# Attention one batch at a time: four kv heads in one transfer of 64 KB a partition and one softmax, where two heads were handled at a time

## The chip, the cores and the metric

The kernel runs on one core of a Trainium2 chip. A core has a matmul engine (TensorE, in the profile PE, and PEld for its weight loads), a vector engine (VectorE, DVE), a scalar engine (ScalarE, ACT), GpSimd (POOL), and SyncE (SP), which here only issues transfers; 16 DMA engines move data from HBM into SBUF, the on-chip memory of 128 partitions. Matmul results go to PSUM, eight banks of 512 float32 a partition. The metric is the device time of one execution in microseconds, the median of several runs; less is better.

## The reference: what is computed

One decode step of a transformer block for 8 batch rows, all weights and caches in bf16. Width D = 1024; 32 query heads on 4 kv heads of 128; a cache of 8192 keys for each batch row and kv head; a gated MLP of F = 3584 with a ReLU gate.

```
mod = (silu(c) @ w_mod) in six parts: sa, ca, ga, sb, cb, gb
h   = layernorm(x) * (1 + ca) + sa
q   = h @ wq                                  # 8 x 32 x 128
s   = q . k_cache * 128**-0.5                 # for each batch row: 32 x 8192
o   = softmax(s) @ v_cache                    # 8 x 32 x 128
x   = x + ga * (o @ wo)
h   = layernorm(x) * (1 + cb) + sb
x   = x + gb * ((relu(h @ W_gate) * (h @ W_up)) @ W_down)
```

K and V are 67.1 MB each; the weights together are 51.4 MB. Each byte is used once.

## The kernel before, in words

**Order and waits.** The kernel is written by hand on a small recorder, `Prog`. `P.op` records an operation for one engine with the ranges that it reads and writes; from these the recorder derives every semaphore wait. Each engine runs its operations in the order recorded. An entry of several matmuls counts as one operation: others can wait for its end alone.

**Transfers.** All large loads go through SyncE's queue, in one order fixed by the list `stream`: w_mod, wq, then K and V of pair 0, K and V of pair 1, and so on, then wo, W_gate, W_up, W_down. `pump` (L381) is called after each recorded TensorE operation. It takes the head of the list if its target range in `arena`, 128 KB a partition, has been read, and records the issue (L393), which then waits for the last readers of that range. `P.held` keeps the range of a K or V transfer from being taken until `free` names the operation that ends its use. The arena is a ring: K or V of a pair takes 32 KB a partition, so four such transfers fit, and K and V have two places each.

**The attention loop** (L683) goes over M = 16 pairs of kv heads, two pairs for one turn of the hardware loop. For a pair m:

- `kt_part` (L586): VectorE transposes an eighth of K in 32x32 blocks into one of four slots of the tile `kt`; the first one waits for K's transfer.
- `qk_part` (L597): four matmuls multiply it with the query weights `qpad` into PSUM; four eighths fill one bank.
- `rowmax` (L609), `spread` (L613, L615), `headmax` (L620, L623): the maximum of the scores of a head, spread over the partitions by a matmul.
- `expo` (L629): ScalarE takes the exponent of two banks, 128x1024, and its sum.
- `p_turn` (L636): VectorE transposes the result in two halves of 64 partitions straight into `pT`, whose zeros keep the two heads of a pair apart.
- `make_qpad` (L578), on GpSimd: query weights of pair m + 2, two places in turn.
- `pv` (L646): 32 matmuls of 512 columns, two at a time on the two halves of the array's columns; waits for V's transfer.
- `fold` (L654, L657), `fold_pe` (L663), `keep` (L668): four masked sums on VectorE, a matmul and a copy bring the result into `oacc`. They are recorded in the middle of pair m + 1, between its transposes and its softmax.

So while TensorE runs PV of one pair, VectorE transposes K of the next, and V of pair m is released by the rowmax of pair m + 1.

**After the loop** come the division by the sums (L706 to L714), turns of the result (L723 to L733), the wo matmuls (L743), the second layernorm (L489 to L508), the gate and up matmuls (L774), and W_down (L793), each of which waits for its part of the weights.

Of the kernel before, what the change touches and what calls it, by code (L numbers as in the profile page):

```python
# [263 lines left out]
def bass_adaLN_cond__gqa_block_cached__glu_gated_reglu__decode_kernel(nc, A_x, A_k_cache, A_v_cache, A_wq, A_wo, B_x, B_W_gate, B_W_up, B_W_down, c, w_mod, out):  # L264
# [11 lines left out]
    SLOT = 8192  # L276
    RING = 16 * 4096
# [13 lines left out]
    with ExitStack() as es:  # L291
# [9 lines left out]
        ktb = sb("kt", [128, NKT * 2048], dt.bfloat16)  # L301
# [5 lines left out]
        jm = sb("jm", [128, 2, J], dt.float32)  # L307
        jms = sb("jms", [128, 2 * J], dt.float32)
        jmp = sb("jmp", [128, 2, J], dt.float32)
        im = sb("im", [128, 4], dt.float32)  # L310
# [10 lines left out]
        M = N // 2  # L321
        qR = sb("qR", [128, 4, M, J], dt.bfloat16)
        rq = sb("rq", [128, 2, 128], dt.bfloat16)
        mq = sb("mq", [128, 4], dt.bfloat16)
        qpad = sb("qpad", [128, 2, 4, 152], dt.bfloat16)
        prb = sb("prb", [128, 1024], dt.bfloat16)
        pT = sb("pT", [128, 2, 32, 2, 32], dt.bfloat16)
        negm = sb("negm", [128, 4], dt.float32)
        mj = sb("mj", [128, 2 * J], dt.float32)
        mjt = sb("mjt", [128, 2 * J], dt.float32)  # L330
        bias = sb("bias", [128, 2], dt.float32)
        lall = sb("lall", [128, M], dt.float32)
        lx = sb("lx", [128, M, 2 * J], dt.float32)
        om = sb("om", [128, Dh], dt.float32)
        oacc = sb("oacc", [128, M + 1, 2 * J], dt.float32)
# [21 lines left out]
        for t in "kv":  # L357
            for i in range(2):
                sems[(t, i)] = E(nc.semaphore("%s_%d" % (t, i)))

        def at(m):

            return m if P.turn is None else 2 * P.turn + m % 2
# [12 lines left out]
        stream, place, cursor = [], {}, [0]  # L376

        def load(key, src, n):
            stream.append((key, src, n))

        def pump():  # L381
            while stream:
                key, src, n = stream[0]
                lo = cursor[0] if cursor[0] + n <= RING else 0
# [3 lines left out]
                cursor[0] = lo + n  # L388
                place[key] = lo
                dst = arena[:, lo:lo + n]  # L390
                if len(src.shape) == 3:
                    dst = dst.rearrange("p (a n) -> p a n", a=src.shape[1])
                P.op("sp", lambda e, dst=dst, src=src: e.dma_start(dst, src), writes=[slot_r(lo, lo + n)], dma=True,  # L393
                     own=(key[0], key[1] % 2) if key[0] in "kv" else None)
# [12 lines left out]
        for i in range(2):  # L407
            load(("wq", i), wq_src[:, 2 * i * SLOT:2 * (i + 1) * SLOT], 2 * SLOT)
# [166 lines left out]
        def make_qpad(m):  # L575
            if m >= M:
                return
# [261 lines left out]
```

## Time and profile before

| | |
|---|---|
| runs, us | 437.17, 445.93, 437.15; median 437.17 |
| profiled execution, its own time | 436.92 us |
| its span (first to last instruction) | 435.6 us |
| TensorE, VectorE, ScalarE, GpSimd busy | 277.4, 265.8, 29.9, 14.5 us |
| bytes read | 185.6 MB, 426 GB/s over the span |
| granted TensorE clock, mean | 0.81 |

A row of the groups reads: line, engine, operation, output <- inputs, shape, count | busy us, mean ns of one | idle time of the engine just before and what ended most of it. A row of the timeline reads: start us, duration us, engine, line, operation, names, shapes, count, with the idle time before it and what ended it in brackets. A row of the windows gives for one stretch the busy time of each engine with its number of instructions, the granted share of the TensorE clock, the busy share of the DMA engines and their GB/s. Line numbers are those of the kernel before.

### The profile page before, as it was taken

Reading aid. Unit: us, or ns where it says so; the run is one execution under the profiler, and the core shown is the slowest. Engines: PE = TensorE matmul, PEld = TensorE weight load, DVE = VectorE, ACT = ScalarE, POOL = GpSimd, SP = SyncE. Lnnn points to the kernel's source line nnn. Section 1 sums busy time; section 2 is a strip of 40 time slices with the busy share of each in tenths; the row PEclk is TensorE's granted clock in tenths of the full one; section 3 lists DMA queues with packets and bytes.
Section 4 is the critical chain, followed back from the end, with each engine's and each line's share of the span. In section 5 each row is a group of like instructions: output and inputs, shape, how many; then the busy total and the mean of one; then the engine's idle time right before and its main releaser. Section 6 shows DMA issues by size and latency. Waiting matters only on the chain.

```text
span 435.6 us, 3869 instructions
## 1 busy us (share of the span) xinstructions
PE 277.4 (64%) x1643; PEld 120.8 (28%) x1483; DVE 265.8 (61%) x377; ACT 29.9 (7%) x62; POOL 14.5 (3%) x32
## 2 busy tenths in 40 slices
PE   0415238659595958768595958768595958636437
PEld 0100002324242423324242333324142323334105
DVE  1503058777686877777778777677788776253020
ACT  2000010110101010010101010010101010110000
POOL 7000000000000000000000000000000000000000
PEclk9966668697888869696978969696987969668858
DMA  9999999999999999999999999999999999999995
GB/s 373 438 444 433 429 433 433 434 430 432 433 433 433 433 433 433 433 433 433 433 433 433 433 433 433 433 433 433 433 433 433 433 433 433 423 429 444 428 420 233
DMA packets 7078, 185.74 MB, mean 426 GB/s; under 512 B 832, under 2 KB 928, under 8 KB 1312
## 3 DMA queue, kind: packets, MB, share of 16 engines
q1 hardware_dynamic: 6944, 185.61, 98.9%
q8 instruction: 5, 0.08, 0.1%
q10 hardware_dynamic: 128, 0.04, 0.0%
q14 instruction: 1, 0.01, 0.0%
HBM read 185.63 MB, written 0.02 MB: 426 GB/s over the span
## 4 chain that ended last, share of the span: by engine, by line
PE 46%; DVE 20%; issue 13%; DMA 6%; ACT 0%; SPq 0%
PE ps L646 22%; PE ps L597 18%; DVE kt L586 9%; DMA arena<-in_B_W_down_dram 6%; DVE negm L609 5%; PE ps L615 2%; PE ps L663 2%; PE ps L743 1%; DVE om L657 1%; DVE mj L620 1%; PE ps L774 1%; DVE mjt L623 1%; DVE negm L613 1%; DVE kt L733 0%; DVE lx L706 0%
## 5 line engine op out<-in xcount | busy, mean ns | idle before, releaser
L586 DVE STREAM_TRANSPOSE kt<-arena 128x1024 uint32<-128x1024 uint32 x128 | 149.6, 1217 | 39.0 <-PE ps L597 26.8
L597 PE MATMUL ps<-kt,qpad 128*128 128x512 bf16 x512 | 122.4, 385 | 9.6 <-DVE kt L586 8.3
L646 PE MATMUL ps<-arena,pT 128*64 128x512 bf16 x512 | 95.4, 554 | 51.7 <-issue 51.7
L646 PEld LDWEIGHTS ps<-arena,pT 128*64 128x64 bf16 x512 | 45.5, 157 | 95.5 <-issue 91.1
L597 PEld LDWEIGHTS ps<-kt,qpad 128*128 128x128 bf16 x512 | 46.0, 97 | 84.6 <-DVE kt L586 28.7
L636 DVE STREAM_TRANSPOSE pT<-prb 64x1024 bf16<-64x1024 bf16 x32 | 39.6, 1239 | 18.1 <-ACT prb L629 17.6
L629 ACT ACTIVATE prb<-ps,bias 128x1024 bf16<-128x1024 f32 x16 | 17.8, 1113 | 293.1 <-DVE mjt L623 293.1
L609 DVE TENSOR_REDUCE negm<-ps 128x1 f32<-128x512 f32 x32 | 22.1, 692 | 12.7 <-PE ps L597 12.7
L663 PE MATMUL ps<-jmp,om 128*128 128x16 f32 x34 | 7.4, 293 | 17.0 <-DVE om L657 17.0
L657 DVE SCALAR_TENSOR_TENSOR om<-ps,im,om 128x128 f32<-128x128 f32 x51 | 17.7, 347 | 0.7
L615 PE MATMUL ps<-identf,negm 128*128 128x128 f32 x32 | 7.8, 326 | 15.6 <-DVE negm L613 15.6
L578 POOL TENSOR_TENSOR qpad<-qR,mq 128x128 bf16<-128x128 bf16 x16 | 6.3, 399 | 317.6 <-DVE pT L636 267.7
L774 PE MATMUL ps<-arena,hT 128*32 128x448 bf16 x128 | 9.4, 459 | 9.4 <-DMA arena<-in_B_W_up_dram 6.8
L544 PE MATMUL ps<-arena,hT 128*32 128x512 bf16 x64 | 7.1, 623 | 12.7 <-DMA arena<-in_A_wq_dram 12.7
L521 PE MATMUL ps<-arena,hT 128*32 128x512 bf16 x96 | 9.2, 565 | 9.2 <-DMA arena<-in_w_mod_dram 9.2
L793 PE MATMUL ps<-arena,hmT 128*32 128x256 bf16 x112 | 8.7, 320 | 5.6 <-DMA arena<-in_B_W_down_dram 5.4
L528 DVE COPY mod<-ps 128x512 f32<-128x512 f32 x2 | 1.3, 671 | 17.8 <-PE ps L521 17.8
L781 DVE TENSOR_TENSOR kt<-ps,kt 128x448 bf16<-128x448 f32 x2 | 1.2, 621 | 17.6 <-PE ps L774 17.6
L663 PEld LDWEIGHTS ps<-jmp,om 128*128 128x128 f32 x34 | 5.7, 210 | 20.5 <-DVE om L657 20.5
L615 PEld LDWEIGHTS ps<-identf,negm 128*128 128x128 f32 x32 | 4.7, 187 | 23.6 <-DVE negm L613 23.6
L555 DVE CAST kt<-ps 128x512 bf16<-128x512 f32 x1 | 0.7, 692 | 16.3 <-PE ps L544 16.3
L793 PEld LDWEIGHTS ps<-arena,hmT 128*32 128x32 bf16 x112 | 6.2, 114 | 9.0 <-DMA arena<-in_B_W_down_dram 7.6
(89 smaller groups left out, 89.2 us busy)
## 6 DMA issues: line engine op xcount, KB each, us to landing
arena<-in_A_k_cache_dram SPq DMA_DIRECT2D x16, 4096.0 KB, 21.1
arena<-in_A_v_cache_dram SPq DMA_DIRECT2D x16, 4096.0 KB, 19.0
arena<-in_A_wq_dram SPq DMA_DIRECT2D x2, 4096.0 KB, 34.9
arena<-in_A_wo_dram SPq DMA_DIRECT2D x2, 4096.0 KB, 18.0
arena<-in_B_W_gate_dram SPq DMA_DIRECT2D x2, 3584.0 KB, 15.5
arena<-in_B_W_up_dram SPq DMA_DIRECT2D x2, 3584.0 KB, 19.0
arena<-in_w_mod_dram SPq DMA_DIRECT2D x1, 6144.0 KB, 30.7
arena<-in_w_mod_dram SPq DMA_DIRECT2D x1, 5888.0 KB, 16.6
```

What stands on the lines that cost most here:

```text
L521: fns.append(lambda e, w=w, pr=pr, j=j, kk=kk: hold(e.matmul(ps[32 * j:32 * j + 32, pr, :], hT[:, kk, :], w[:, 2 * pr:2 * pr + 2, j, :], s ...
L586: P.op("dve", lambda e: e.transpose(ktb[:, to:to + QE].bitcast(dt.uint32), arena[:, lo:lo + QE].bitcast(dt.uint32)), reads=[slot_r(lo, lo ...
L597: fns.append(lambda e, t=t, r=r: e.matmul(ps[:, b, :].rearrange("p (c k) -> p c k", k=32), qpad[:, m % 2, t * 2 + r, 24 - 8 * i:152 - 8 * ...
L609: P.op("dve", lambda e: e.tensor_reduce(negm[:, h:h + 1], ps[:, b, :], AX.X, ALU.max, negate=True), reads=[bank(b)] + (free(("v", m - 1)) ...
L615: P.op("pe", lambda e: e.matmul(ps[:, 4, 0:128], negm[:, 2:3].to_broadcast([128, 128]), identf[:], start=True, stop=True), reads=[R("negm" ...
L629: P.op("act", lambda e: e.activation(prb[:], ps[:, 2 * z:2 * z + 2, :].rearrange("p h n -> p (h n)"), ACT.Exp, bias=bias[:, z:z + 1], scal ...
L636: P.op("dve", lambda e, g=g: e.transpose(pT[64 * g:64 * g + 64, z, :, g, :], prb[64 * g:64 * g + 64, :]), reads=[R("prb")] + ([R("qpad", z ...
L646: fns.append(lambda e, t=t: e.matmul(ps[64 * (t % 2):64 * (t % 2) + 64, 5, :].rearrange("p (i d) -> p i d", d=Dh), pT[:, z, t].rearrange(" ...
L657: P.op("dve", lambda e, i=i: e.scalar_tensor_tensor(out=om[:], in0=ps[:, 5, Dh * i:Dh * i + Dh], scalar=im[:, i:i + 1], in1=om[:], op0=ALU ...
L663: P.op("pe", lambda e: e.matmul(ps[:, 6 + z, 0:16], om[:], jmp[:].rearrange("p g j -> p (g j)"), start=True, stop=True), reads=[R("om"), R ...
L774: fns.append(lambda e, w=w, r=kk - r0, kk=kk, h=h, j=j, b0=b0: hold(e.matmul(ps[32 * j:32 * j + 32, b0 + h, 0:H], hT[:, kk, :], w[:, r, j, ...
L793: fns.append(lambda e, w=w, r=k - r0, k=k, i2=i2, j=j: e.matmul(ps[32 * j:32 * j + 32, 4, 0:256], hmT[:, k, 1 - i2:33 - i2], w[:, r, i2, j ...
```

## The change

Attention goes over the 8 batches in place of 16 pairs, one turn of the hardware loop each. K of all four kv heads of a batch is one transfer of 64 KB a partition (8.4 MB), V another. The arena grows to 144 KB a partition with fixed places: K at 0, a staging area of 16 KB behind it, V behind that; each of K and V has one place. GpSimd copies the last quarter of K (parts 12 to 15 of 16) into the staging area as soon as K has landed, so that K's place is free after part 11 has been transposed and the copy is done; its release is named by the first rowmax, recorded after part 12. There is one softmax maximum over four banks, two exponents (f = 0, 1), and the turn of P is one transpose of 128 partitions followed by four masked copies, which write `pT` in the place of `kt`. PV has twice as many matmuls of half as many columns. The two folds of a batch are recorded at its own end, and release V. QK of parts 0 and 1 is one recorded operation. wq is loaded in parts of six and two eighths (it was halves), gate, up and wo in one transfer each; up goes where wo lay and W_down where gate lay.

The core of the diff:

```diff
-    SLOT = 8192
-    RING = 16 * 4096
+    SLOT = Sk * G * Dh // 128
+    PART = SLOT // 16
+    STAGE, VPART, RING = SLOT, SLOT + 4 * PART, 2 * SLOT + 4 * PART
...
-        pT = sb("pT", [128, 2, 32, 2, 32], dt.bfloat16)
+        pT = ktb.rearrange("p (f c i g x) -> p f c i g x", f=2, c=32, i=2, g=G)
...
-        for i in range(2):
-            load(("wq", i), wq_src[:, 2 * i * SLOT:2 * (i + 1) * SLOT], 2 * SLOT)
-        for m in range(M):
-            for nm, t in (("k", A_k_cache), ("v", A_v_cache)):
-                load((nm, m), t[m // 2, 2 * (m % 2):2 * (m % 2) + 2].rearrange("g (p c) d -> (g p) (c d)", p=64), 2 * SLOT)
-        wo_parts = [(0, 16), (16, 32)]
...
+        wq_parts = [(0, 6), (6, 8)]
+        for i, (r0, r1) in enumerate(wq_parts):
+            load(("wq", i), wq_src[:, r0 * 4096:r1 * 4096], (r1 - r0) * 4096, 48 * D if i == 0 else STAGE)
+        for b in range(B):
+            for nm, t, lo in (("k", A_k_cache, 0), ("v", A_v_cache, VPART)):
+                load((nm, b), t[b].rearrange("g (p c) d -> (g p) (c d)", p=32), SLOT, lo)
+        load(("wo", 0), wo_src, KO * D, 0)
+        load(("gate", 0), g_src, KC * F, VPART)
+        load(("up", 0), u_src, KC * F, 0)
...
+        def kt_part(b, e):
+            lo = e * PART if e < 12 else STAGE + (e - 12) * PART
+            to = e % NKT * PART
+            P.op("dve", lambda e_: e_.transpose(ktb[:, to:to + PART].bitcast(dt.uint32), arena[:, lo:lo + PART].bitcast(dt.uint32)),
...
+        def set_aside(b):
+            lo = 12 * PART
+            P.op("pool", lambda e: e.tensor_copy(arena[:, STAGE:STAGE + 4 * PART].bitcast(dt.uint32),
+                                                 arena[:, lo:lo + 4 * PART].bitcast(dt.uint32)),
+                 reads=[R("landed"), slot_r(lo, lo + 4 * PART)], writes=[slot_r(STAGE, STAGE + 4 * PART)])
...
+        def rowmax(b, h):
+            P.op("dve", lambda e: e.tensor_reduce(negm[:, h:h + 1], ps[:, h, :], AX.X, ALU.max, negate=True),
+                 reads=[bank(h)] + (free(("k", b)) if h == 0 else []), writes=[R("negm", h, h + 1)])
...
-        def p_turn(m):
-            z = m % 2
-            for g in range(2):
-                P.op("dve", lambda e, g=g: e.transpose(pT[64 * g:64 * g + 64, z, :, g, :], prb[64 * g:64 * g + 64, :]),
+        def p_turn(b, f):
+
+            P.op("dve", lambda e: e.transpose(pd[:, f], prb[:, f]), reads=[R("prb", f, f + 1)], writes=[R("pd", 1024 * f, 1024 * f + 1024)])
+            for g in range(G):
+                P.op("dve", lambda e, g=g: e.tensor_scalar(out=pT[:, f, :, :, g, :], in0=pd[:, f].rearrange("p (c i x) -> p c i x", c=32, i=2),
+                                                           scalar1=mqf[:, g:g + 1], scalar2=None, op0=ALU.mult),
...
+        def pv(b, f):
...
+            for n in range(64):
+                h, c_, i, t = n // 32, n // 2 % 16, n % 2, n % 2
+                fns.append(lambda e, n=n, h=h, c_=c_, i=i, t=t: e.matmul(
+                    ps[64 * t:64 * t + 64, 5, 0:2 * Dh].rearrange("p (i d) -> p i d", d=Dh),
+                    pT[:, f, 16 * h + c_, i].rearrange("p g x -> p (g x)"), vv[:, f, h, c_, 2 * i:2 * i + 2],
...
+        def fold(b):
+            for i in range(2):
+                P.op("dve", lambda e, i=i: e.tensor_scalar(out=om[:, i], in0=ps[:, 5, Dh * i:Dh * i + Dh], scalar1=im[:, i:i + 1],
+                                                           scalar2=None, op0=ALU.mult),
+                     reads=[bank(5), R("im")] + (free(("v", b)) if i == 0 else []), writes=[R("om", i, i + 1)])
...
-        for m in range(M):
-            P.trip = m // 2
-            for e8 in range(8):
-                kt_part(m, e8)
-                qk_part(m, e8)
-                if e8 == 5:
-                    rowmax(m, 0)
-            fold(m - 1, 0)
-            fold(m - 1, 1)
-            rowmax(m, 1)
-            spread(m)
-            fold(m - 1, 2)
-            headmax(m)
-            expo(m)
-            fold(m - 1, 3)
-            fold_pe(m - 1)
-            keep(m - 1)
-            p_turn(m)
-            make_qpad(m + 2)
-            pv(m)
+        for b in range(B):
+            P.trip = b
+            kt_part(b, 0)
+            set_aside(b)
+            kt_part(b, 1)
+            qk_parts(b, (0, 1))
+            for e in range(2, 16):
+                kt_part(b, e)
+                qk_parts(b, (e,))
+                if e >= 12 and e < 15:
+                    rowmax(b, e - 12)
+            rowmax(b, 3)
+            headmax(b)
+            for f in range(2):
+                expo(b, f)
+            for f in range(2):
+                p_turn(b, f)
+                if f == 0:
+                    make_qpad(b + 1)
+                pv(b, f)
+            fold(b)
```

In the changed kernel the transposes of K are on line 573, the copy aside on 579, QK on 592, the rowmax on 598, the exponent on 614, the turn of P on 620, the masked copies on 622, PV on 632, the folds on 641, and the issues on 390. The masks `jm`, `jmp` and `im` are laid out for four heads, the query weights are taken from the turned q by one copy in place of a matmul and four copies, and the wo, gate and up matmuls wait once for all their weights.

## The prediction

> **What bounds the kernel now.** I read the page first (DMA row, chain), then the windows of the attention loop, then one iteration on the timeline, then SyncE's waits and the completion times of the transfers.
>
> From the page: the span, the clock and DMA rows by fortieths of the span, and the chain by engine.
>
> ```profile
> span 435.6 us, 3869 instructions
> ...
> PEclk9966668697888869696978969696987969668858
> DMA  9999999999999999999999999999999999999995
> ...
> PE 46%; DVE 20%; issue 13%; DMA 6%; ACT 0%; SPq 0%
> ```
>
> The chain names TensorE with 46%, but the DMA row is full in 39 of 40 slices. The windows say which of the two is real (columns: busy time of each engine, granted clock, DMA share, GB/s):
>
> ```profile
> 80.00:176.00 96.00, 70.55 (x340) 31.20 (x340) 73.16 (x100) 6.39 (x15) 1.59 (x4) 0.84 1.00 432
> 176.00:334.00 158.00, 113.95 (x544) 50.19 (x544) 119.96 (x162) 10.22 (x24) 3.59 (x9) 0.85 1.01 434
> 177.50:182.20 4.70, 4.66 (x24) 2.35 (x25) 3.71 (x4) 0.00 (x0) 0.00 (x0) 0.51 0.98 425
> 183.40:189.00 5.60, 5.40 (x27) 2.24 (x26) 4.31 (x5) 0.00 (x0) 0.00 (x0) 1.00 0.98 421
> ```
>
> The DMA engines have no gap at 432 to 434 GB/s. The K transfers complete at 62.24, 81.57, 100.91, 120.23 us, 19.36 apart, so a batch (two pairs of kv heads, 16.8 MB) costs 38.72; each of the first nine iterations starts its transposes 0.13 us after such a completion. The last W_down transfer completes at 432.59, the span ends 3.0 later, and the execution's own time is 436.92, 1.3 over its span and 0.25 under the median of 437.17. So **the transfers bound it, from start to end**; the engines follow 0 to 3 us behind.
>
> Why there is no gap: SyncE issues a transfer when its buffer is free, and it waits for that about 10 us at a time:
>
> ```profile
> SPq L393 <- DVE negm L609: 168.9, 15, 11.9
> SPq L393 <- DVE pT L636: 137.1, 16, 22.4
> ```
>
> (engine and line, whom it waited for: us in total, times, longest), and the page's list of DMA issues, whose last column is the time from issue to landing:
>
> ```profile
> arena<-in_A_k_cache_dram SPq DMA_DIRECT2D x16, 4096.0 KB, 21.1
> arena<-in_A_v_cache_dram SPq DMA_DIRECT2D x16, 4096.0 KB, 19.0
> ```
>
> A transfer of 9.7 us lands 19 to 21 us after its issue: it stood 9 to 11 us behind another. That queue is the margin that the change spends.
>
> **What the change does to the transfers.** The same bytes go in half as many issues. Removed issues cost nothing now: each is 0.33 us of SyncE, beside full queues. The rate of longer rows: w_mod's 48 KB rows took 1.815 us a row and engine, the caches' 32 KB rows 1.213: 433 and 432 GB/s. I count no gain and no loss. The Trainium skill (SBUF — State Buffer, "The DMA setup-cost knee") gives every transfer about 2 us that do not grow with its bytes and advises the largest single transfer; by that 16 issues fewer would save 32 us, but only of transfers that stand alone, and the DMA share of 1.00 says that none does. The skill's first page (Trainium Kernel Development and Optimization, "Best Practices") says to double-buffer, which speaks against this change: K and V now have one buffer each.
>
> So the question is when a buffer is free. K(b+1) is issued after the transposes of parts 0 to 12 and the first rowmax (parts 12 to 15 are copied aside), V(b+1) after the first fold of batch b. Order in the queue: K(b), V(b), K(b+1), V(b+1). With S the start of a batch's transposes, K(b+1) has left the queue at S+38.2. From an issue to its first packet 1.3 us pass (second w_mod transfer: 0.64 to 1.93). So V(b+1) must be issued by **S+36.9**, or the DMA engines stand idle.
>
> **The new path of one batch**, by the rows of this iteration:
>
> ```profile
> 168.10 2.36 DVE L586 STREAM_TRANSPOSE kt<-arena 128x1024 uint32<-128x1024 uint32 x2
> ...
> 171.59 0.69 DVE L609 TENSOR_REDUCE negm<-ps 128x1 f32<-128x512 f32 x1 [0.52 <-PE ps L597]
> ...
> 174.93 2.51 DVE L636 STREAM_TRANSPOSE pT<-prb 64x1024 bf16<-64x1024 bf16 x2 [1.10 <-ACT prb L629]
> ...
> 177.54 5.90 PE L646 MATMUL ps<-arena,pT 128*64 128x512 bf16 x32 [3.26 <-issue]
> ...
> 178.49 4.62 DVE L586 STREAM_TRANSPOSE kt<-arena 128x1024 uint32<-128x1024 uint32 x4 [1.04 <-DVEq L181]
> ```
>
> - 16 transposes at 4.62/4 = 1.155: 18.5. Three rowmaxes among them at 0.61 (0.69, of which 0.08 overlap): 1.8.
> - A stall at the start. QK of parts 0 and 1 is one operation of 8 matmuls. TensorE has idled since the last PV and runs at 0.51 of its clock, 0.427 us a matmul (0.216 at 1.00): it ends at S+2.4+3.4 = 5.8, while the fifth transpose, which reuses the first of four slots, could start at S+4.6: 1.2.
> - From the last transpose's end (170.46) to the rowmax: 1.1. Rowmax 0.7. From its end to the turn of P (172.28 to 174.93): 2.65. S+26.0 is reached.
> - Turn of P, first half: one transpose of 1024 bf16, 1.24 (L636), then four masked copies (new L622, 128x1024 bf16), which the trace doesn't have. Rows on both sides:
>
> ```profile
> L636 DVE STREAM_TRANSPOSE pT<-prb 64x1024 bf16<-64x1024 bf16 x32 | 39.6, 1239 | 18.1 <-ACT prb L629 17.6
> L532 DVE TENSOR_SCALAR mod<-mod 128x256 f32<-128x256 f32 x2 | 0.6, 294 | 0.1
> L481 DVE TENSOR_SCALAR sel<-dsel 128x128 f32<-128x128 f32 x1 | 0.2, 222 | 0.0
> ```
>
>   Below: 0.22, a tensor_scalar that is all fixed cost; above: 1.24, a pass over 1024 elements. L481 and L532 grow by 0.56 ns an element, so 0.73; it is the same operation, so I take it, 0.06 less back to back: 4 x 0.67 = 2.7. The bounds move the path by -1.8 and +2.0. The Trainium skill (VectorE: DVE Perf Modes, "The perf-mode tier table") has a bf16 tensor_scalar in SBUF at 693 ns for 2048 elements, four a cycle; by it a copy would be some 0.43 (an estimate), the path 1.2 shorter and the sum below about 10 us lower. No row here has a 16-bit one.
> - PV of both halves: 64 pairs of 256-column matmuls, at 0.1065 to 0.11 a pair when warm (half of 0.216; W_down's 256-column pairs on L793 start 0.109 apart) 7.0. TensorE has idled over 5 us, so it starts cold: each PV of before ran cold for 3.2 to 6.3 us (totals 5.0, 5.9, 6.35, 6.58 against 3.5), and 1 us of cold costs 0.49: mean 5.1, +2.5. The 128 weight loads double in number; L793's loads are hidden at this pace, so nothing for them. The second half's turn (3.9) lies beside the first half's PV. With 0.1 to start: 9.6.
> - Last matmul to the end of the first fold (L654 0.31, semaphore): 0.45.
>
> Sum: 18.5+1.8+1.2+1.1+0.7+2.65+1.24+2.7+9.6+0.45 = 39.9, **S+40.0** with rounding, 3.1 us after S+36.9. The second fold and the loop's turn add 0.4 (between two iterations 0.03 us passed at 295.57, but now the branch follows a wait), and the next K has landed: the period is **P = 40.4**, no longer set by the transfers (38.72). Before, transposes of one pair ran beside PV and folds of the other; that overlap is what goes.
>
> Hidden: the copy aside on GpSimd, 4096 words at 0.84 ns (L449, L450: 283 and 390 ns for 128 and 256) 3.6 us, due at S+16; even three times that is covered, and GpSimd's 0.40 us operation at 176.25 didn't stretch the transposes beside it. K(b+1)'s issue at S+1.2+15.0+0.6 = S+17 comes just before V(b) ends. make_qpad has 10 us.
>
> **Start and end.** wq's second part is issued at 36.3 instead of 22.5, beside a longer first part that lands at about 45.7: covered by 9 us. K(0) lands where K and V of the first pair did, 71.9, S(0) = 72.1. After the last fold at 72.1+7P+P-0.4, gate (its region holds V) waits for it: 1.3, then gate, up, W_down of 7.34 MB at 433 GB/s, 16.94 each: 50.8; up waits for the wo matmuls and W_down for gate's, both before the queue is empty. Then 0.3 to completion, 3.0 of tail, 1.3 over the span. Total = 128.4 + 8P: for 40.4 **452 us**. (For 38.72 it gives 438, the time before plus the one gap.)
>
> **Rivals.**
> 1. *The transfers stay the bound*: not slower. Mechanism: the path from S to the first fold fits into 36.9. For it: copies at the lower bound (-1.8), a warm QK start (-1.2), the short cold stretch (-0.8) together give 36.2. Against: all three are needed, and the clock of 0.51 stands at every PV of before. It decides at S+36.9, 437 to 438; up to P = 39.6 it is partly so, within 2% (445). Chance 0.20, of which 0.02 for faster, since a gain could come from the tail alone.
> 2. *The copies run at an element a cycle*, 1.2 each, or PV pays for its doubled weight loads: P = 42.3, 467; with the longest cold stretch 473. For: the output is cut into runs of 16 elements. Against: L532's slope. 0.18.
> 3. *64 KB rows transfer more slowly*, so the change does not do what it says: 3% on the caches' 310 us, about 461. Against: w_mod's rows. 0.05.
>
> Forecast (P 39.8 to 41.3, 447 to 459): 0.57. Slower by over 2%, about what a measurement can tell from no change: 0.57+0.18+0.05 = 0.80; same 0.18; faster 0.02. The range 443 to 469 leaves out most of rival 1's lower half and rival 2's end, under 2 in 10.
>
> **What would show it.** DMA share in the loop about 38.7/40.4 = 0.96, with gaps ahead of each V; SyncE's wait for the fold (L641) before each V issue; transposes starting every 40.4 us, right after a fold and not after a completion; the clock at 0.5 twice a batch; L622 near 0.7. Wrong would be: transposes that wait for K with a DMA share of 1.00 (rival 1), L622 over 1 us (rival 2), or gaps at the K issues.

## The result and the profile after

The changed kernel takes **454.84 us** (median of 452.14, 453.93, 455.75 and 459.02), the kernel before 437.16 beside it: **1.0385 times the time, 95% interval 1.0319 to 1.0452**. The forecast was 452 in a range of 443 to 469, slower. The sign and the size came out; one step of the mechanism did not, and most of what follows is about that step.

The page of the changed kernel: span, the rows of the granted clock and of DMA by fortieths of the span, the chain by engine, and the groups of the transposes, of the masked copies and of make_qpad.

```profile
span 457.7 us, 4771 instructions
...
PEclk9976575797798779788888979988796789777667
DMA  9999999999989898999989989998999998999995
...
DMA 9%; PE 6%; DVE 5%; issue 0%; ACT 0%; ACTq 0%
...
L573 DVE STREAM_TRANSPOSE kt<-arena 128x1024 uint32<-128x1024 uint32 x128 | 148.4, 1211 | 38.7 <-DVEq L181 28.7
...
L622 DVE TENSOR_SCALAR kt<-pd,mqf 128x1024 bf16<-128x1024 bf16 x64 | 28.2, 504 | 0.6
...
L564 POOL TENSOR_TENSOR qpad<-qR,mq 128x128 bf16<-128x128 bf16 x8 | 4.9, 606 | 215.3 <-DVE kt L622 158.9
```

Before, the DMA row was full in 39 of 40 slices; now it has eights in it from a quarter of the span to its end. The windows give the size (columns: busy time of each engine, granted clock, DMA share, GB/s). The first is the loop, the second six microseconds about the issue of V(2):

```profile
80.00:361.50 281.50, 194.22 (x1385) 104.51 (x1386) 195.55 (x252) 17.30 (x34) 29.57 (x14) 0.83 0.97 411
158.00:164.00 6.00, 3.22 (x35) 2.10 (x30) 4.21 (x6) 0.20 (x1) 2.29 (x1) 0.81 0.66 251
```

411 GB/s instead of 432 to 434, and a stop in which DMA falls to 0.66. The timeline of one batch (start in us, duration, engine, line):

```profile
198.16 0.61 DVE L641 TENSOR_SCALAR om<-ps,im 128x128 f32<-128x128 f32 x2 [5.76 <-PE ps L632]
198.53 0.33 SPq L390 DMA_DIRECT2D arena<-in_A_v_cache_dram  x1
...
201.30 4.62 DVE L573 STREAM_TRANSPOSE kt<-arena 128x1024 uint32<-128x1024 uint32 x4 [2.53 <-DVEq L181]
...
207.36 10.25 DVE L573 STREAM_TRANSPOSE kt<-arena 128x1024 uint32<-128x1024 uint32 x9 [1.44 <-PE ps L592]
...
218.22 0.33 SPq L390 DMA_DIRECT2D arena<-in_A_k_cache_dram  x1
...
228.54 1.87 DVE L622 TENSOR_SCALAR kt<-pd,mqf 128x1024 bf16<-128x1024 bf16 x4
...
230.47 8.56 PE L632 MATMUL ps<-arena,kt 128*64 128x256 bf16 x128 [5.13 <-DVE kt L622]
...
239.08 0.61 DVE L641 TENSOR_SCALAR om<-ps,im 128x128 f32<-128x128 f32 x2 [5.80 <-PE ps L632]
...
239.46 0.33 SPq L390 DMA_DIRECT2D arena<-in_A_v_cache_dram  x1
...
241.67 1.25 DVE L573 STREAM_TRANSPOSE kt<-arena 128x1024 uint32<-128x1024 uint32 x1 [1.98 <-DVEq L181]
```

The waits of SyncE and of VectorE (engine and line, whom it waited for: us in total, times, longest):

```profile
SPq L390 <- DVE om L641: 171.1, 8, 22.3
SPq L390 <- DVE negm L598: 166.6, 8, 40.0
...
DVE kt L573 <- DVEq L181: 28.7, 8, 18.2
```

Each V is issued 0.03 us after a first fold has ended, as forecast. But the transposes do not follow the fold: they sit 2 us until 201.30 and 241.67, and K landed at 201.16 and 241.52. In seven of the eight batches of this execution the transposes start 0.14 to 0.15 us behind a landing of K (in batch 2, where K had landed before the second fold ended, 0.28), on the mean every 40.23 us. So both sides wait for each other: V for the end of the chain of computations, and the next chain for the K that stands behind that V in the queue.

Where the 22.1 us between the two spans (435.6, 457.7) lie: 7.9 up to the landing of the first K (79.80 instead of 71.91, see below), 10.7 from there to the landing of K(7), 3.3 from K(7) to the last of W_down (V(7), gate), 0.2 in the tail. The 7.9 are a disturbance, not the change: three of the four profiles of the changed kernel show executions whose transfers ran at 388 GB/s through the first 57 us, where the fourth and the kernel before have 428, and the ratios of times leave such executions out. Profiles without it, those of the changed kernel and of its variants alike, have the first K at 71.7 to 72.2.

### The profile page after: what moved, and what is told of

The parts are those of the page before. It is cut to its first block, busy times and chain, and to the rows that moved or that the text cites. A ratio compares the mean times of both kernels' runs of the same rounds, so it can differ in the third digit from the quotient of the medians.

```text
span 457.7 us, 4771 instructions
## 1 busy us (share of the span) xinstructions
PE 267.9 (59%) x2135; PEld 138.7 (30%) x1975; DVE 249.8 (55%) x340; ACT 29.3 (6%) x53; POOL 37.5 (8%) x30
## 5 line engine op out<-in xcount | busy, mean ns | idle before, releaser
L592 PE MATMUL ps<-kt,qpad 128*128 128x512 bf16 x512 | 140.8, 421 | 64.6 <-DVE kt L573 62.1
L573 DVE STREAM_TRANSPOSE kt<-arena 128x1024 uint32<-128x1024 uint32 x128 | 148.4, 1211 | 38.7 <-DVEq L181 28.7
L632 PE MATMUL ps<-arena,kt 128*64 128x256 bf16 x1024 | 72.5, 315 | 40.9 <-DVE kt L622 40.9
L592 PEld LDWEIGHTS ps<-kt,qpad 128*128 128x128 bf16 x512 | 47.9, 105 | 155.1 <-DVE kt L573 96.7
L632 PEld LDWEIGHTS ps<-arena,kt 128*64 128x64 bf16 x1024 | 65.3, 129 | 47.5 <-DVE kt L622 42.4
L579 POOL COPY arena<-arena 128x4096 uint32<-128x4096 uint32 x8 | 28.8, 3597 | 112.1 <-DVE kt L573 112.1
L641 DVE TENSOR_SCALAR om<-ps,im 128x128 f32<-128x128 f32 x16 | 4.9, 347 | 50.4 <-PE ps L632 50.4
L622 DVE TENSOR_SCALAR kt<-pd,mqf 128x1024 bf16<-128x1024 bf16 x64 | 28.2, 504 | 0.6
L620 DVE STREAM_TRANSPOSE pd<-prb 128x1024 bf16<-128x1024 bf16 x16 | 19.8, 1239 | 10.9 <-ACT prb L614 10.9
L518 DVE COPY mod<-ps 128x512 f32<-128x512 f32 x2 | 1.3, 670 | 20.3 <-PE ps L511 20.3
L743 PEld LDWEIGHTS ps<-arena,hT 128*32 128x32 bf16 x64 | 2.2, 133 | 22.9 <-DMA arena<-in_B_W_up_dram 12.6
L604 PE MATMUL ps<-identf,negm 128*128 128x128 f32 x16 | 3.9, 326 | 7.8 <-DVE negm L602 7.8
## 6 DMA issues: line engine op xcount, KB each, us to landing
arena<-in_B_W_down_dram SPq DMA_DIRECT2D x1, 3584.0 KB, 20.3
```

The lines of the kernel that those rows point to most:

```text
L573: P.op("dve", lambda e_: e_.transpose(ktb[:, to:to + PART].bitcast(dt.uint32), arena[:, lo:lo + PART].bitcast(dt.uint32)), reads=[slot_r(l ...
L579: P.op("pool", lambda e: e.tensor_copy(arena[:, STAGE:STAGE + 4 * PART].bitcast(dt.uint32), arena[:, lo:lo + 4 * PART].bitcast(dt.uint32)) ...
L592: fns.append(lambda e_, t=t, r=r, i=i, kv=kv, h=e // 4: e_.matmul(ps[:, h, :].rearrange("p (c k) -> p c k", k=32), qpad[:, t * 2 + r, 24 - ...
L620: P.op("dve", lambda e: e.transpose(pd[:, f], prb[:, f]), reads=[R("prb", f, f + 1)], writes=[R("pd", 1024 * f, 1024 * f + 1024)])
L622: P.op("dve", lambda e, g=g: e.tensor_scalar(out=pT[:, f, :, :, g, :], in0=pd[:, f].rearrange("p (c i x) -> p c i x", c=32, i=2), scalar1= ...
L632: fns.append(lambda e, n=n, h=h, c_=c_, i=i, t=t: e.matmul(ps[64 * t:64 * t + 64, 5, 0:2 * Dh].rearrange("p (i d) -> p i d", d=Dh), pT[:, ...
```

## The experiments

Theories, as they stood after the first comparison. **A**: the batch has one place for V and one for K, each released late; the issues come too late for the queue, DMA stops, and the chain waits for what comes late. **B**: the chain of computations alone sets the period, as the prediction had it. **C**: the 64 KB rows, or having few large transfers, cost the time.

To read the runs, I take the loop from the landing of the first K to that of the last (of the second half, where K came in two; in the kernel before, from the landing of V of its first pair to that of its fifteenth, by which as many bytes have come), 271.0 us before, and for each K and V transfer two numbers from the completion times of its 16 engines: its **margin**, from its issue to the mean end of the transfer ahead of it, and its **loss**, the mean end of it minus that of the one ahead minus the time of its bytes at full rate (19.36 us for 64 KB a partition, 9.68 for 32). The **chain** is the time from a batch's first transpose to the end of its first fold.

### The changed kernel again

> The changed kernel once more, for a profile to set the others against. In its first profile K(0) landed at 79.80 us, 7.9 later than the 71.9 forecast, because the transfers up to 57 us ran at 385 GB/s instead of 433; the loop behind it ran in 40.23 us a batch. Every theory expects 452 to 456 us as the median. If the slow start was a disturbance of that one execution, transposes of batch 0 begin near 72 us, the period stays at 40.0 to 40.4 us, and the span comes to 450 to 453 us; if the start belongs to the change, they begin at 80 us again.

> The changed kernel once more, since both of its profiles so far show executions at the upper end of its times (459.0 and 458.0 us of 450.6 to 459.0). Of the 16 DMA engines the first and the last ended a K transfer 2.0 to 3.5 us apart through most of the second profile and 0.55 to 0.6 us apart in most of the first, with periods of 41.1 and 40.2 us. Theory A expects 450 to 456 us, a period of 39.9 to 40.6 us, transposes of batches 1 to 7 that start 0.1 to 0.2 us behind K's landing, and an idle stretch of DMA ahead of each V.

> The changed kernel beside these two: 450 to 456 us. Its loop again with transposes that wait for K, 39.9 to 41.1 us a batch.

Measured: 453.61 us (450.61 to 457.97), 1.036 times before, 95% 1.0316 to 1.0404; then 450.73 and 460.90; then 452.86 and 462.33. The second profile's first K landed at 71.66 us and its transposes began at 71.80, 0.3 before the forecast: the late first K does not belong to the change. The periods of the four profiles are 40.23, 41.10, 40.53 and 40.55. All four are of executions of 458 to 462 us, above the kernel's medians, so these periods may be on the long side; the late control in the next experiment was profiled at 454.84 and has 40.82. In the second, engines ended a K transfer up to 3.5 us apart, and its last engine's landing released the transposes; by that much such a batch is longer. A chain that waits for each landing pays for the slowest of 16 engines at every transfer. That the executions of this kernel scatter (450.6 to 458.0 in one set) where 15 of the kernel before, beside these kernels, lay from 436.5 to 437.2 fits this; it was not tested by itself.

### V in two halves, the first released early

```diff
-            for nm, t, lo in (("k", A_k_cache, 0), ("v", A_v_cache, VPART)):
-                load((nm, b), t[b].rearrange("g (p c) d -> (g p) (c d)", p=32), SLOT, lo)
+            load(("k", b), A_k_cache[b].rearrange("g (p c) d -> (g p) (c d)", p=32), SLOT, 0)
+            for f in range(2):
+                load(("vw"[f], b), A_v_cache[b].rearrange("g (p c) d -> (g p) (c d)", p=32)[:, f * HALF:f * HALF + HALF], HALF,
+                     VPART + f * HALF)
...
-            P.op("pe", fns, reads=[slot_r(VPART, VPART + SLOT), ("kt", 4096 * f, 4096 * f + 4096)], writes=[bank(5)],
-                 own_wait="v" if f == 0 else None)
+            P.op("pe", fns, reads=[slot_r(VPART + f * HALF, VPART + f * HALF + HALF), ("kt", 4096 * f, 4096 * f + 4096)]
+                 + (free(("v", b)) if f == 0 else []), writes=[bank(5)], own_wait="vw"[f])
...
-                     reads=[bank(5), R("im")] + (free(("v", b)) if i == 0 else []), writes=[R("om", i, i + 1)])
+                     reads=[bank(5), R("im")] + (free(("w", b)) if i == 0 else []), writes=[R("om", i, i + 1)])
```

> V of a batch comes in two transfers of 32 KB a partition, into the same place; the first one's place is released when the first half of the PV products has read it, about 4.3 us before the fold, the second's by the fold as now. Theory A (V has one place, it is released only at the end of the batch's own chain, so DMA idles before each V, and K, issued behind V, comes late by as much): the idle stretch of 1.1 to 1.8 us ahead of V goes, the period falls from 40.23 to the transfers' own 38.7, 8 x 1.5 = 12 us are saved: 440 to 444 us, and transposes still wait for K's landing. Theory B (the batch's chain of computations is the bound, as the prediction had it): the chain is as long as before, so 450 to 455 us. Theory C (the time comes from the 64 KB rows or the few large transfers): only V's transfers are halved, so about half of the 17 us come back, 446 to 448 us.

The control has the same two transfers, both released by the fold:

```diff
-                 + (free(("v", b)) if f == 0 else []), writes=[bank(5)], own_wait="vw"[f])
+                 writes=[bank(5)], own_wait="vw"[f])
...
-                     reads=[bank(5), R("im")] + (free(("w", b)) if i == 0 else []), writes=[R("om", i, i + 1)])
+                     reads=[bank(5), R("im")] + (free(("v", b)) + free(("w", b)) if i == 0 else []), writes=[R("om", i, i + 1)])
```

> V of a batch in the same two transfers of 32 KB a partition, but both released by the fold, where the one is now. It separates the size of the transfers from the moment of release. Theories A and B: no change, 452 to 456 us, the same idle stretch ahead of V. Theory C (the size of the rows or the number of transfers costs the time): as much as two halves released early bring, 440 to 448 us.

Measured: **447.00 us** with the early release (1.0274 times before, 1.0207 to 1.0341) and **455.48** with the late one (1.043, 1.0404 to 1.0455). The windows of the two loops, early and late:

```profile
72.00:349.00 277.00, 191.22 (x1384) 102.76 (x1384) 195.63 (x252) 17.28 (x34) 29.58 (x14) 0.86 0.99 422
72.00:357.50 285.50, 196.00 (x1386) 105.40 (x1386) 195.57 (x252) 17.48 (x35) 29.57 (x14) 0.83 0.97 410
```

The same rows and the same number of transfers differ by 8.5 us by the moment of release alone, and the late one is where the changed kernel is: theory C falls as far as V's rows go. B falls too. The chain is 38.0 us on the mean of the early run and 38.7 in the late one, which by B is worth some 5 us, and in both the periods (39.58 and 40.82) are 1.0 and 1.6 us longer than the chain and the 0.57 from its first fold to the next transpose, because transposes wait for K. A is right in kind, and the time is 3 us above its 440 to 444. Waits of SyncE in the run with early release (engine and line, whom it waited for: us in total, times, longest):

```profile
SPq L390 <- DVE negm L601: 158.5, 8, 37.5
SPq L390 <- PE ps L635: 122.6, 7, 18.6
SPq L390 <- DVE om L644: 45.9, 8, 21.1
```

V's first half now waits for the first PV half (L635), and the fold (L644) no longer has 171 us of SyncE's waiting but 46. What is left is the first row: K, released by the first row maximum; 6.6 of the 7.4 us that the transfers still lose are K's.

### A longer chain

```diff
             P.op("dve", lambda e: e.transpose(pd[:, f], prb[:, f]), reads=[R("prb", f, f + 1)], writes=[R("pd", 1024 * f, 1024 * f + 1024)])
+            for i in range(2 if f == 0 else 0):
+                P.op("dve", lambda e, i=i: e.transpose(junk[:, i], prb[:, f]), reads=[R("prb", f, f + 1)],
+                     writes=[R("junk", i, i + 1)])
             for g in range(G):
```

> Two more transposes of 128x1024 bf16 (1.24 us each in the trace) ahead of the first masked copy of each batch, into a tile that nobody reads: the chain from the batch's first transpose to its fold is 2.5 us longer, from about 38.4 to 40.9. Theory A: a batch starts when K lands, 41.2 us after the fold of the batch before the last, so two periods are the chain plus 41.2: (40.9 + 41.2)/2 = 41.05, and at least the chain plus some 0.4 us for the turn to the next batch, 41.3; against 40.23 now that is 1.1 us a batch, 9 us in all: 461 to 465 us, with the wait for K before the transposes gone or under 0.3 us. Theory B (the chain alone sets the period): 2.5 us a batch, 20 us in all: 472 to 476 us. If the transfers alone set the period: no change, 452 to 456 us.

Measured: **461.16 us** (1.0529, 1.0446 to 1.0611), 7.5 over the changed kernel of the same set where B has 20 and transfers alone nothing. The chain to the fold is 39.8 to 41.1 us; the transposes now follow the fold by 0.56 to 0.95 us, and V is issued 0.5 us ahead of the end of the transfer before it at best, 2.8 us behind it at worst. Waits of VectorE:

```profile
DVE kt L574 <- DVEq L181: 19.2, 8, 15.9
```

15.9 us of it are the wait for the first K, so 3.3 are left for seven batches, against 10.5 in the changed kernel (28.7, of which 18.2 the first). A longer chain first eats the wait for K. The changed kernel stands near the edge between two bounds: here the wait is all but gone, and the period of 41.10 is the chain and its turn. That any further microsecond would count in full was not tested.

### A shorter chain

```diff
+        def spin(n):
+            P.op("pe", [lambda e: e.matmul(ps[:, 7, :], identb[:], hmT[:].rearrange("p k r -> p (k r)")[:, 0:512], start=True, stop=True)
+                        for i in range(n)], reads=[R("identb"), r_hmT], writes=[bank(7)])
...
             rowmax(b, 3)
+            spin(4)
             headmax(b)
+            spin(26)
...
             fold(b)
+            spin(16)
```

> Matmuls into a bank that nobody reads keep TensorE busy where it idled: 4 ahead of the head maximum, 26 behind it, 16 behind the fold; nothing that is used changes. The granted clock should then stay at 1.0 into the PV products and the first QK products: PV 7.0 to 7.5 us instead of 8.5 to 9.9, the stall of the first transposes on TensorE 0.3 us instead of 1.4, the chain to the fold 2.5 to 3 us shorter, 35.5 instead of 38.3. Theory A (a microsecond of the chain is half a microsecond a batch): 1.25 to 1.5 us a batch, 10 to 12 us in all, near the transfers' own 38.7: 442 to 446 us. If the chain set the period alone: 2.5 to 3 us a batch until the transfers' 38.7 is the bound, the same 442 us. If DMA lost its time by itself (its slow first packets after a stop, whatever the chain): no gain, 450 to 456 us.

Measured: **447.62 us** (1.0265, 1.0236 to 1.0295). The rows of the clock and the group of PV:

```profile
PEclk9976655999999999989999999999899999987668
...
L632 PE MATMUL ps<-arena,kt 128*64 128x256 bf16 x1024 | 57.4, 273 | 0.0
```

The clock stays up, PV takes 7.18 us in each batch and the chain 35.6 to 36.0 from the second batch on: the steps of the forecast on a cold TensorE were right. But 2.7 us off the chain bring some 6 us in all by the medians, 0.75 a batch, and less than the expected 442 to 446. The transposes now begin 3.4 to 4.5 us behind the fold, waiting for K. V was issued 1.4 to 3.1 us before DMA needed it and still lost up to 1.3 us: the time that I had allowed from issue to need was too short.

### K released earlier too

```diff
                 kt_part(b, e)
                 qk_parts(b, (e,))
+                if e == 11:
+                    P.op("dve", lambda e_: e_.tensor_copy(mark[:], arena[:, STAGE:STAGE + 2]),
+                         reads=[slot_r(STAGE, STAGE + 2)] + free(("k", b)), writes=[R("mark")])
...
-                 reads=[bank(h)] + (free(("k", b)) if h == 0 else []), writes=[R("negm", h, h + 1)])
+                 reads=[bank(h)], writes=[R("negm", h, h + 1)])
```

> V in two halves, and K released 2.4 us earlier, by a one-column copy behind the twelfth transpose in place of the first row maximum (batch's start + 14.6 us instead of 17.0). In the run of V in halves alone 3.1 us of the 277.1 from the first K's landing to the last's were idle and packets longer than 2.42 us (65,536 bytes) or 1.21 us (32,768) took another 3.9; K was issued 17 us behind K's landing, while the engines ended V 17.3 to 19.4 us behind it. If K's late issue is what is left of the loss, the period goes from 39.6 to 38.7-38.9 us: 439 to 442 us. If what is left lies with the 64 KB rows themselves, no gain on the 447.0 us of V in halves alone.

Then gate in two transfers on top of it, each part with its own matmuls:

```diff
-        load(("gate", 0), g_src, KC * F, VPART)
+        for i in range(2):
+            load(("gate", i), g_src[:, 4 * i * F:4 * (i + 1) * F], 4 * F, VPART + i * HALF)
...
-        for nm, b0 in (("gate", 0), ("up", 2)):
+        for nm, i, b0, r0, r1 in (("gate", 0, 0, 0, 4), ("gate", 1, 0, 4, 8), ("up", 0, 2, 0, 8)):
```

> The same, and gate in two transfers of 28 KB a partition, each issued when its half of V's place is released, 4.3 us apart. In the kernel with V in halves no idle stretch stood ahead of gate; in the second profile of the changed kernel one of 2.3 us did. Theory A: every transfer is issued ahead of need again, so the transfers are the bound from the first to the last: 437 to 440 us, equal to the kernel before within 1%. It can't be faster than before, where they were the bound already.

Measured: **443.73 us** (1.0159, 1.0144 to 1.0173) with K earlier, **442.09** (1.0106, 1.0081 to 1.0131) with gate in halves as well. Both miss their ranges by about 2 us, in the same direction as the run before. In the first of the two profiles K's issue had 1.8 to 4.3 us of margin and lost 0.7 on the mean, V's first half 2.2 to 4.1 and 0.3. V's second half, with 8.7 or more, lost nothing.

### K released later

```diff
-            lo = e * PART if e < 12 else STAGE + (e - 12) * PART
+            lo = e * PART
...
-                 reads=[bank(h)] + (free(("k", b)) if h == 0 else []), writes=[R("negm", h, h + 1)])
+                 reads=[bank(h)] + (free(("k", b)) if h == 2 else []), writes=[R("negm", h, h + 1)])
...
-            set_aside(b)
...
-                if e >= 12 and e < 15:
+                if e >= 12 and e < 14:
                     rowmax(b, e - 12)
+            rowmax(b, 2)
```

> No copy aside: parts 12 to 15 of K are read in place, so K is released behind the last transpose, about 22 us behind the batch's start instead of 17, 2.6 us after DMA has ended V. The chain to the fold keeps its length. Theory A: K lands at 22 + 2.1 (issue to first packet) + 19.4 + 0.2 = 43.7 us behind the start, which is the period; V's issue at 38.4 is then early enough. 43.8 against 40.5 us a batch and once more for the last: 474 to 484 us. If the chain of computations set the period, K's issue could be late without cost: 450 to 456 us.

Measured: **476.87 us** (1.0915, 1.0895 to 1.0935), period 43.61. The page's DMA row is open now, once a batch:

```profile
DMA  9999999689969986996999699889978996999986
```

From the third batch on, K issued 2.4 to 2.8 us late loses 4.5 to 4.9 us; V, with 3.9 to 5.3 us of margin, loses nothing (-0.06 to 0.12). The chain, 37.7 to 39.1 us, is as long as it was. So the copy on GpSimd, 3.6 us and hidden, is worth 23 us, and it is K's release that it buys.

### K in halves: both released in time

```diff
+            for nm, t, c0, c1, lo in (("k", A_k_cache, 0, SLOT // 2, 0), ("j", A_k_cache, SLOT // 2, SLOT, SLOT // 2),
+                                      ("v", A_v_cache, 0, SLOT, VPART)):
+                load((nm, b), t[b].rearrange("g (p c) d -> (g p) (c d)", p=32)[:, c0:c1], c1 - c0, lo)
...
-                 writes=[("kt", to, to + PART)] + ([R("landed")] if e == 0 else []), own_wait="k" if e == 0 else None)
+                 writes=[("kt", to, to + PART)] + ([R("landed")] if e == 8 else []), own_wait="k" if e == 0 else "j" if e == 8 else None)
...
-                 reads=[bank(h)] + (free(("k", b)) if h == 0 else []), writes=[R("negm", h, h + 1)])
+                 reads=[bank(h)] + (free(("j", b)) if h == 0 else []), writes=[R("negm", h, h + 1)])
...
+            for e in range(16):
+                kt_part(b, e)
+                if e == 8:
+                    set_aside(b)
+                    P.op("dve", lambda e_: e_.tensor_copy(mark[:], im[:, 0:1]), reads=[R("im")] + free(("k", b)), writes=[R("mark")])
+                else:
+                    qk_parts(b, (8, 9) if e == 9 else (e,))
+                if e >= 12 and e < 15:
+                    rowmax(b, e - 12)
```

> K of a batch in two transfers of 32 KB a partition, V still in one of 64 KB released by the fold. Transposes begin when the first half of K has landed, 9.7 us before the second; the fold then comes about 28.7 us behind the landing of all of K, and V is issued some 10 us before DMA has ended the transfers ahead of it; each half of K's place is released long before it is needed. In the ten profiles so far a transfer issued at least 5 us ahead of the mean end of the one before it lost nothing (-0.05 to 0.08 us), one issued at that end lost 2.2 us, and up to 3.8 us ahead some lost up to 1.3. Theory A (the issues come too late): no transfer loses time, the period is 38.7 to 38.9 us, 436.5 to 439 us, equal to the kernel before, with V's rows still at 64 KB. Theory of the rows (64 KB rows cost time): V's eight transfers keep their loss, 443 us or more. The batch's chain as the bound: chain 38.4 and a turn of 0.5 give 38.9 a batch, no more than 2 us over theory A, so this run doesn't tell those two apart.

Measured: **436.53 us**, 0.9989 times the kernel before, 95% 0.998 to 0.9999. From its page, the span and the DMA row, full again:

```profile
span 435.6 us, 4795 instructions
...
DMA  9999999999999999999999999999999999999995
```

Its window from the first whole K to the last (columns as above):

```profile
72.00:342.60 270.60, 185.21 (x1388) 103.19 (x1386) 196.67 (x259) 17.49 (x35) 29.62 (x14) 0.89 1.00 434
```

All of the loss is gone, with V still in one transfer of 64 KB rows and one place each for K and V. The chain of 37.5 to 39.1 us now begins when half of K has landed, 9.7 us earlier by the transfers' clock, and that is margin for both: V's issue has 7.7 to 8.8 us, K's halves 16 and 20, and no transfer loses more than 0.16. K's rows are 32 KB here, but 64 KB rows of K cost nothing either where they were issued in time: with 4 us of margin or more they lost -0.05 to 0.12 us (11 transfers in seven other profiles). The large batch of the change is not what costs; when it lets its places go is. No slack is left in the chain, though: in four of the seven later batches the transposes begin 0.32 us behind the second fold, with the half of K landed 0.6 us or more before, so the chain with its turn takes as long as the transfers.

### A balance over all transfers

All K and V transfers of the thirteen profiles, sorted by margin (248; left out are the first K of each, and the first V of the three executions whose first K came at 79.7 us or later):

| issued ahead of the mean end of the transfer before, us | transfers | mean loss, us | smallest to largest |
|---|---|---|---|
| -4.1 to -0.5 | 16 | 3.98 | 2.69 to 6.30 |
| -0.5 to 0.5 | 17 | 2.03 | 1.65 to 2.88 |
| 0.5 to 1.5 | 17 | 1.29 | 0.97 to 1.73 |
| 1.5 to 2.5 | 38 | 0.72 | -0.04 to 1.74 |
| 2.5 to 4 | 44 | 0.19 | -0.04 to 1.15 |
| 4 to 5 | 15 | 0.00 | -0.06 to 0.12 |
| over 5 | 101 | 0.00 | -0.05 to 0.16 |

The kernel before is in the last line alone (5.7 us at the least). And by kernel:

| | first K landed | loop | last K to last W_down | sum of losses | time, median |
|---|---|---|---|---|---|
| before | 71.91 | 270.97 | 89.70 | 0.1 | 436.87 |
| changed, first profile | 79.80 | 281.63 | 93.04 | 14.2 | 454.84 |
| changed, second profile | 71.66 | 287.71 | 94.24 | 17.1 | 453.61 |
| V in halves, late | 71.80 | 285.72 | 92.98 | 15.8 | 455.48 |
| chain longer | 71.81 | 287.72 | 95.38 | 19.8 | 461.16 |
| chain shorter | 72.00 | 279.26 | 91.94 | 9.7 | 447.62 |
| V in halves, early | 71.94 | 277.09 | 91.68 | 7.4 | 447.00 |
| and K earlier | 72.08 | 276.95 | 92.13 | 7.0 | 443.73 |
| and gate in halves | 72.19 | 276.17 | 92.41 | 5.5 | 442.09 |
| K later | 71.96 | 305.28 | 95.71 | 35.8 | 476.87 |
| K in halves | 71.97 | 270.66 | 89.94 | 0.0 | 436.53 |

The third and fourth profiles of the changed kernel have loops of 283.69 and 283.84 us and losses of 16.3 and 14.2; in the first, third and fourth 2.0 to 2.4 us of that are the V left out above. Profiles are single executions and the times are medians, so the columns agree to a few us, not to one. But the order of the losses is that of the times, the three rows near 454 us apart. The sums take in the last V, which lands behind the loop: without it the losses give the loop's excess over the kernel before within 1.5 us in every row (second profile of the changed kernel: 15.6 lost, the loop 16.7 longer).

## Why the prediction was right in size and wrong in one step

- **What bounds before, and where the change spends it: right.** Transfers from start to end; the change spends the margin in the queue. K in halves gives the margin back, and the time with it.
- **No gain from fewer issues, none lost by long rows: right.** 65,536-byte packets take 2.418 us as median, 32,768-byte ones 1.213; V in halves, released late, changes nothing. The Trainium skill (SBUF — State Buffer, "The DMA setup-cost knee") has about 2 us a transfer that do not grow with its bytes: here a transfer that is issued when the one ahead ends does lose 2.0 on the mean, and one that is issued 5 us ahead loses nothing. In the kernel before, all K and V transfers together lost 0.1 us, so 16 issues fewer had nothing to save, and the 2 us came where the issues came late. The double-buffering that the skill's first page (Trainium Kernel Development and Optimization, "Best Practices") asks for gave the kernel before its margin of 5.7 us or more; K in halves has 7.7 or more with one place each.
- **The path of a batch: right but for two terms.** Transposes with their stalls were to end at S+21.5 and end there in most batches of the first profile (S+20.3 at the earliest); the turn of P starts at S+25.96 (26.0). The four masked copies take 1.87, so 0.47 each, and not 2.7: the 16-bit rate that the skill's table gives (VectorE: DVE Perf Modes, "The perf-mode tier table", 0.43 by estimate) was nearer than the slope of the 32-bit rows, 0.67. PV takes 9.06 on the mean of eight (8.5 to 10.0) in place of 9.6. Together the fold ends at S+38.4, not S+40.0. The copy aside (3.597 us on its row, 3.6 forecast) is hidden; make_qpad takes 0.61 us beside the masked copies instead of 0.40 and is hidden too. One spread is misread: by the prediction's own rows the cold stretch costs from 0.9 us less to 0.6 more than its mean, while the sums of rivals 1 and 2 take 0.8 either way; that moves their ends by under 2 us.
- **"From an issue to its first packet 1.3 us pass", and V is due at S+36.9: the 1.3 held, but it is not all that a late issue costs.** Twelve 64 KB transfers were issued 0.26 to 4.1 us behind the mean end of the one ahead. Their first packets started 1.1 to 1.3 us after the issue (mean of the 16), but took 0.7 us longer than 2.42 on the mean, and a landing comes 0.3 us behind its last packet: so such a transfer loses 2.1 to 2.2 us on top of its lateness (2.5 once). What the expectation for K released later calls 2.1 from issue to first packet is that sum. And even 2 us ahead of the end some lose 1.3, so S+36.9 was too late. This also fells **"K(b+1)'s issue at S+17 comes just before V(b) ends"**, which the sum counted at nothing: K's margin was 0.8 to 5.6 us in the four profiles of the changed kernel, and it lost 0.3 to 0.75 us a batch beside V's 1.1 to 1.7.
- **"The next K has landed: the period is P = 40.4, no longer set by the transfers": the step that failed.** It has not landed. V goes out at the fold, the K behind it 38.7 us and two losses later; in the first profile the transposes of the next batch but one began 41.3 to 41.5 us after a fold in four cases of six, 43.2 and 43.7 in the others (two transfers 38.7, first packets 1.2 after the issue, 0.7 by which they are slow, 0.3 to the landing, the spread of the engines, 0.14 to the first transpose, and K's own loss where there is one). So two periods are the chain plus 41.3 or more: (38.4 + 41.3)/2 = 39.85 at the least, 40.2 to 41.1 measured. That the forecast's 40.4 agrees with this is luck: a chain 1.6 us too long stood in place of a wait for K that it did not have. The chain alone would give 38.4 + 0.5 = 38.9 and, by the formula of the prediction, 440 us: its mechanism with the right terms would have said "same". The longer chain (0.38 us a batch for each microsecond by the medians, not 1) and the shorter one (0.28) show the difference, though executions that scatter by some us leave these two slopes rough.
- **After the last fold:** 56.7 us to the end of the execution were forecast, 59.1 and 59.4 passed; the first packets of gate behind a stop, and V(7)'s lateness, are in it.
- **What would show it:** DMA share 0.97 (0.96), stops ahead of V, SyncE's wait for L641 (171 us in all): seen. Losses at the K issues, named there as a sign against it: seen too, the smaller part. Transposes right after a fold: not seen, they followed a completion, which stood there as a sign of the rival with the transfers as the bound, together with a DMA share of 1.00. The case in between, transfers that wait for computations that wait for transfers, was not among the rivals.

## What to carry to other kernels

A place that holds a whole batch ties its release to the end of the batch's chain; what counts is how long before the queue runs dry that release comes. For transfers of this size an issue should stand 4 to 5 us ahead of the end of the one before it, not merely ahead of it. And where the consumer of one transfer releases the place of another, write the period over both buffers, as a loop of waits: the sum of one chain can be off in its slope by a factor of two and more even where its value happens to fit. Before giving up a large batch, let its first consumer start on half of it and release each half by itself: here that took back the whole 17 us.

## What was not expected of the hardware

- After a stop, the first 65,536-byte packets take longer: in the second profile the 14 that start between 111.0 and 111.9 us took 2.7 to 3.7 us instead of 2.42. In that loop nearly as much is lost to slow packets (7.9 us) as to idle engines (9.2). Also with 2 to 3 us of margin single packets took up to 4.3 us (the shorter chain); in the kernel before, with the next transfer always queued, three of 4,608 packets of 32,768 bytes were over 10% longer than the median. Why margins of 2 to 4 us sometimes cost nothing and sometimes 1.3 us stays open.
- The 16 engines end one transfer 2.0 to 2.1 us apart throughout the kernel before. Behind an issue 0.2 us or more late they end 0.4 to 0.8 us apart (1.8 once); in the second profile of the changed kernel, where only one issue was that late, the spread of the others was 0.5 to 3.5.
- PV's 128 weight loads of 128x64 are hidden behind 256-column matmuls: with the clock up, 128 of them take 7.18 us, 0.056 each.
